# Delta-rule attention and two gated feed-forward layers on one core: seven of sixteen second products in rounded parts, the weights' sign by a steeper negative slope, the second chunk's masks as VectorE products

## The chip, the cores and the metric

One NeuronCore of a Trainium2 chip runs the whole program. The metric is the device time of one execution in microseconds (us). Before the change three runs gave a median of 1096.58 us (1095.71 to 1097.54).

## The reference, cut to what matters

Inputs are q, k, v of shape (4, 8, 768, 48), beta (4, 8, 768), and the weights of two feed-forward layers in 64-bit floats.

```python
k_n = k / (norm(k) + 1e-6)
for t in range(768):                                   # per batch and head
    y[t]  = q[t] @ state
    state = state + beta[t] * outer(k_n[t], v[t] - state.T @ k_n[t])
x = y as (3072 tokens, 384)
h = x @ w_in                                           # layer 1: 384 -> 2048
g = (a0 + a1*h + a2*h**2 + a3*h**3) / (1 + |b0|*|h| + |b1|*h**2 + 1e-6)
x = g @ w_out                                          # 2048 -> 384
h = x @ w_in2; g = max(h, 0)**2; out = g @ w_out2      # layer 2
```

## The kernel before, in words

**Attention** is cut into 12 chunks of 64 time steps by 4 batches: 48 steps n, in six groups of eight (two chunks each). Within a chunk the recurrence is solved by inverting a triangular matrix; that inversion is a chain of 31 pairs of small operations (lines 487 and 491), on VectorE for group 0 and on GpSimd for the others. A step multiplies keys and queries with the state, masks the query-key product to the part above the diagonal, and multiplies on. The mask is made in `middle` (line 679): ScalarE or VectorE copies the product out of PSUM into the tile X (line 691, printed at the helper's lines 345 and 349), and GpSimd zeroes the rest in place (`affine_select`, line 690). X goes into the matmuls of lines 711 and 712.

**The layers** work on six token tiles of 512 columns. A tile has 16 steps j, one for each 128 of the 2048 hidden units. In layer 1 a step is `mm1` (nine matmuls, line 896, into one of three PSUM banks "h"), `rational` (ScalarE, VectorE and one GpSimd product, lines 913 to 923, whose result g goes into one of three buffers) and `mm2_1` (line 933: three products in full fp32, which the trace shows as two matmuls each, added to three PSUM banks over the 16 steps). Layer 2 has the same `mm1`, then `relu2`, then `mm2_2` (lines 957 to 959). There, as in every `mm1`, an operand is split into a rounded part (fp32r) and the remainder, and a product is three matmuls on rounded numbers: high by low, low by high, high by high.

**The weights** come as 64-bit floats, 768 KB per step j and layer, into a "raw" buffer. `weights` (line 811) makes 32-bit floats of them in place: ScalarE scales the high words (line 836, which moves the exponent), VectorE shifts the low words (837), VectorE puts the sign of the high word into the low one (838), VectorE shifts and joins (841 and 843 for layer 1, 847 for layer 2). Then ScalarE rounds (852, 861) and GpSimd forms the remainder (853, 862). In layer 1 eight weights have room of their own and the others share two raw buffers. For layer 2, j = 0 and 1 are loaded into the same two raw buffers in tile 0 and joined early; j = 2 goes into a buffer that exists only after `swap` (line 975), which frees the attention's memory; four lie in quarters of B, once tile 5 of layer 1 has used those for the last time.

**The order of the work** is not the program's text. Every piece of work is a task with an engine, a modelled duration, a due time and its predecessors. `Plan.play` is a list scheduler that simulates all queues, `Plan.late` derives new due times from a simulated schedule, and `Plan.run` takes the best of eight rounds. So each engine's queue is fixed before the chip runs, and each engine works through its queue in order. Constants such as `T0`, `U1` (planned us per step of layer 1), `STEP0`, and the lead of the second layer's weights (100 - 5.5 j us) only set the first due times. `either` leaves a copy to ScalarE or VectorE as the scheduler likes.

Attention of group i+1 and the inversion of group i+2 run beside tile i of layer 1. The prologue, before the first `mm1`, has the attention of group 0 and the inversion of group 1.

Of the kernel before, what the change touches and what calls it, by code (L numbers as in the profile page):

```python
# [19 lines left out]
C = 64  # L20
# [8 lines left out]
N = 2 * CT  # L29
EPS = 1e-6  # L30

T0, U1, U2 = 88.0, 6.0, 4.15
T2 = T0 + 96 * U1 + 3
STEP0, STEP1, INV0, INV1 = 40, 25, -90, -10
GD, GN = 40, 28
ROUNDS, FILL = 8, 0
PREF = 1.0
IV1, WB, WS = 25, 44, 4.5

# [204 lines left out]
def kernel(ctx, tc, kT, kS, qT, kn, vn, beta, par_in, w1, w2, outT):  # L244
# [31 lines left out]
    tiles(one, "raw", 2, [128, 2 * DM], w1.dtype)  # L276
# [33 lines left out]
    mark = at.tile([128, 1, 1], F32, name="mark")  # L310
    be = at.tile([128, 32], F32, name="be")
# [45 lines left out]
    add("POOL", 0.2, lambda: P_.memset(tiny, 1e-30), w=["tiny"])  # L357

# [81 lines left out]
    def attention(g):  # L440
# [238 lines left out]
        def middle(k, due):  # L679
# [3 lines left out]
            for j in range(2):  # L683
# [127 lines left out]
    def weights(l, j, due, duo, slack):  # L811
# [7 lines left out]
        wait = [] if l == 1 or not 1 < j < 8 or j == 3 else [PL.last["late"]] if j < 3 else free2[4 * (j - 4) + 3]  # L819
        over = [i for k in (6, 7) if l == 1 and 4 * (k - 4) <= j < 4 * (k - 3) for i in used["raw", 1, k]]  # L820
        dma(768 if f64 else 384, lambda: raw(rk), src[j], w=[rk, (rk, 1)], due=2 + 2 * j if e and l == 1 else d0 - 10, alloc=None if e else (("raw",), rk), lat=2.2, after=[used["load"]] + wait if l == 2 else [],
# [84 lines left out]
    def rational(i, j, due):  # L906
# [173 lines left out]
```

## Time and profile before

| | us |
|---|---|
| median of three runs | 1096.58 |
| the profiled execution's own time | 1095.48 |
| its span, first to last instruction | 1093.8 |
| TensorE busy | 1034.8 (95%) |
| VectorE, ScalarE, GpSimd busy | 722.0, 615.4, 438.8 |
| mean granted TensorE clock | 0.970 |
| prologue, to the first L896 | about 98 |
| tiles 0 to 5 of layer 1, to the last L933 | 98 to 692.7 |
| layer 2 | 692.7 to the end |

PE is TensorE's matmuls, PEld its weight loads, DVE VectorE, ACT ScalarE, POOL GpSimd, SP the DMA queue. L933 is line 933 of the kernel. The ends of matmuls are modelled, so two that follow each other overlap in the listing: the time of a group is read from the start of one to the start of the next.

### The profile page before, as it was taken

The numbers are of one execution on the slowest core, as the hardware profiler recorded it, in microseconds if no ns is written. First come the engines' busy times: TensorE is split into PE (matmuls) and PEld (weight loads), VectorE is DVE, ScalarE is ACT, GpSimd is POOL, SyncE is SP. The second block draws the span as 40 slices with busy tenths as digits, with TensorE's granted clock in tenths as the row PEclk, the third lists the DMA queues.
The fourth block names the chain that finished last, engine by engine and source line by source line (L and its number), as shares of the span: only waits on it lengthen the run. The fifth ranks groups of instructions, "written<-read, shape, count | busy, mean of one in ns | idle before, by whom it ended". The sixth has DMA issues, their size and how long they took to land.

```text
span 1093.8 us, 22125 instructions
## 1 busy us (share of the span) xinstructions
PE 1034.8 (95%) x8843; PEld 743.4 (68%) x8843; DVE 722.0 (66%) x1164; ACT 615.4 (56%) x1106; POOL 438.8 (40%) x592
## 2 busy tenths in 40 slices
PE   6768898799999999999999899999999999999998
PEld 5656566466666666666666555688888888888886
DVE  4986788799788769767878699894343343433432
ACT  5454776576776777766777588663333232332422
POOL 2398899469628835862232334551000000000000
PEclk7869899899999999999999999999999999999999
DMA  7771536811650381043010321811001010000000
GB/s 238 202 185 54 131 115 205 205 55 38 155 94 34 108 165 47 23 113 64 33 32 8 103 71 31 303 42 47 11 14 44 1 58 1 1 30 1 29 1 29
DMA packets 126022, 85.42 MB, mean 78 GB/s; under 512 B 93344, under 2 KB 110880, under 8 KB 125920
## 3 DMA queue, kind: packets, MB, share of 16 engines
q1 hardware_dynamic: 125920, 84.02, 28.0%
q8 instruction: 69, 1.13, 0.4%
q14 instruction: 33, 0.27, 0.1%
HBM read 64.20 MB, written 18.61 MB: 76 GB/s over the span
## 4 chain that ended last, share of the span: by engine, by line
PE 68%; POOL 10%; DVE 6%; ACT 4%; issue 2%; DMA 1%; SPq 0%; POOLq 0%; ACTq 0%
PE bank L896 31%; PE bank L933 15%; PE bank L959 6%; PE bank L957 6%; PE bank L958 6%; POOL Tt L491 3%; PE bank L652 3%; POOL tmp L487 3%; POOL mem L916 3%; ACT X L345 1%; PE bank L711 1%; POOL A L853 1%; DVE mem L917 1%; DVE mem L350 1%; DVE mem L918 1%
## 5 line engine op out<-in xcount | busy, mean ns | idle before, releaser
L896 PE MATMUL bank<-xh,A 128*128 128x512 f32 x1152 | 361.6, 395 | 3.3 <-POOL A L853 3.3
L933 PE MATMUL bank<-mem,B 128*128 128x512 f32 x576 | 273.1, 607 | 4.6 <-DVE mem L923 4.6
L896 PE MATMUL bank<-xl,A 128*128 128x512 f32 x576 | 257.1, 446 | 15.0 <-DVE mem L923 11.3
L896 PEld LDWEIGHTS bank<-xh,A 128*128 128x128 f32 x1152 | 218.9, 190 | 65.5 <-issue 14.9
L916 POOL TENSOR_TENSOR mem<-mem 128x512 f32<-128x512 f32 x96 | 126.5, 1318 | 186.8 <-ACT mem L914 186.4
L933 PEld LDWEIGHTS bank<-mem,B 128*128 128x128 f32 x576 | 106.5, 192 | 101.2 <-issue 85.7
L945 DVE SCALAR_TENSOR_TENSOR mem<-bank,mem 128x512 f32<-128x512 f32 x96 | 66.2, 689 | 145.9 <-ACT mem L944 145.8
L896 PEld LDWEIGHTS bank<-xl,A 128*128 128x128 f32 x576 | 109.4, 190 | 63.3 <-DVE mem L923 14.7
L944 ACT ACTIVATE mem<-bank 128x512 f32<-128x512 f32 x96 | 57.4, 598 | 147.7 <-PE bank L896 147.7
L957 PE MATMUL bank<-gl,C 128*128 128x512 f32 x288 | 113.6, 395 | 0.5 <-DVE gl L948 0.5
L948 DVE TENSOR_TENSOR gl<-mem,gh 128x512 fp32r<-128x512 f32 x96 | 71.9, 749 | 63.6 <-ACT gh L947 63.4
L959 PE MATMUL bank<-gh,C 128*128 128x512 f32 x288 | 113.8, 395 | 0.0
L958 PE MATMUL bank<-gh,C 128*128 128x512 f32 x288 | 112.0, 389 | 0.0
L947 ACT CAST gh<-mem 128x512 fp32r<-128x512 f32 x96 | 59.6, 621 | 82.9 <-DVE mem L945 71.4
L919 ACT ACTIVATE mem<-mem,par 128x512 f32<-128x512 f32 x96 | 69.3, 722 | 54.4 <-POOL mem L916 53.9
L491 POOL TENSOR_TENSOR Tt<-Tt,tmp 128x31 f32<-128x31 f32 (+15 forms) x155 | 93.6, 604 | 10.8
L921 DVE SCALAR_TENSOR_TENSOR mem<-mem,par,bank 128x512 f32<-128x512 f32 x96 | 71.3, 743 | 38.1 <-ACT bank L920 37.9
L487 POOL TENSOR_TENSOR tmp<-Gb,Tt 128x31 f32<-128x31 f32 (+15 forms) x155 | 88.2, 569 | 14.1 <-DVE Tt L480 3.9
L913 ACT ACTIVATE mem<-bank 128x512 f32<-128x512 f32 x96 | 57.0, 593 | 57.4 <-PE bank L896 42.4
L914 ACT ACTIVATE mem<-mem,par 128x512 f32<-128x512 f32 x96 | 78.0, 813 | 2.7
L345 ACT COPY X<-bank 64x192 f32<-64x192 f32 (+1 forms) x187 | 63.0, 338 | 28.9 <-DVE vn L695 12.9
L917 DVE TENSOR_TENSOR mem<-bank,mem 128x512 f32<-128x512 f32 x96 | 65.9, 687 | 17.7 <-ACT mem L345 15.7
(117 smaller groups left out, 1579.8 us busy)
## 6 DMA issues: line engine op xcount, KB each, us to landing
raw<-in_w_dram SPq DMA_DIRECT2D x18, 768.0 KB, 4.8
B<-in_w_dram SPq DMA_DIRECT2D x10, 768.0 KB, 5.2
kTg<-in_kS_dram SPq DMA_DIRECT2D x40, 128.0 KB, 2.9
gs<-Gs SPq DMA_DIRECT2D x40, 128.0 KB, 2.8
kTc<-in_kT_dram SPq DMA_DIRECT2D x40, 128.0 KB, 2.6
kn<-in_kn_dram SPq DMA_DIRECT2D x12, 384.0 KB, 3.8
X<-in_qT_dram SPq DMA_DIRECT2D x96, 48.0 KB, 2.7
vn<-in_vn_dram SPq DMA_DIRECT2D x12, 384.0 KB, 4.3
```

Of the source, the lines that this page charges most:

```text
L345: A_.copy(a, b) if f is None else A_.mul(a, b, f) if g is None else A_.activation(a, b, AF.Identity, bias=f, scale=g)
L487: E_.tensor_tensor(tv, _mid(Gb[:, s, s + 1:32], [128, a, b]), Tt[:, 0:a, s:s + 1].to_broadcast([128, a, b]), op=ALU.mult)
L491: E_.tensor_tensor(Tt[:, 0:a, s + 1:32], Tt[:, 0:a, s + 1:32], tv, op=ALU.subtract)
L896: M.matmul(h, a, b, start=(k == 0 and m == 0), stop=(k == NK - 1 and m == 2))
L914: add("ACT", 0.83, lambda: A_.activation(b(), a(), AF.Identity, bias=s(4), scale=s(5)), r=[ak, "par"], w=[bk], due=due + 3.3, alloc=(("b", ...
L916: add("POOL", 1.32, lambda: P_.tensor_tensor(b(), b(), a(), op=ALU.mult), r=[ak], w=[bk], due=due + 4.2, lock=1)
L917: add("DVE", 0.69, lambda: V.tensor_tensor(c(), h(), c(), op=ALU.mult), r=[hk], w=[ck], due=due + 5.5)
L933: M.matmul(acc[d], Bw[j][:, 128 * d:128 * d + 128], slot[gk], start=(j == 0), stop=(j == NJ - 1))
L948: add("DVE", 0.72, lambda: V.tensor_tensor(gl(), b(), gh(), op=ALU.subtract), r=[bk, gk, "late"], w=[lk], due=due + 5, lock=1, alloc=(("gl ...
L957: M.matmul(acc[d], wh, gl, start=(j == 0), stop=False)
L958: M.matmul(acc[d], wl, gh, start=False, stop=False)
L959: M.matmul(acc[d], wh, gh, start=False, stop=(j == NJ - 1))
```

## The change

1. For tiles 1 to 5 of layer 1 and the seven steps j in `SJ`, `mm2_1` becomes nine matmuls on rounded parts. ScalarE rounds g (tile ph), GpSimd forms the remainder (tile pl); there is one buffer of each. The weights' parts E and F are made once, in tile 1: seven roundings on ScalarE, seven subtractions on GpSimd. Their memory is that of the two raw buffers and free space, given over by the task `pairs` once all weights of layer 1 are done.
2. The scaling of the high words becomes a parametric ReLU whose negative slope is larger by 2**32. The sign then stands where the later shift by 3 puts it at the top, and the VectorE operation of line 838 goes, for all 32 weights.
3. In chunk 1 (steps n = 4 to 7, in the prologue) one VectorE product of PSUM and a constant triangle `tri` replaces the copy and GpSimd's mask. `tri` is made once on GpSimd.
4. Layer 2 no longer uses layer 1's raw buffers: its weights j < 4 and j > 7 use two new buffers after `swap`, with a planned lead of 60 - 4 j us. `U1` is 5.9 and `STEP0` 36.

```diff
-T0, U1, U2 = 88.0, 6.0, 4.15
+T0, U1, U2 = 88.0, 5.9, 4.15
-STEP0, STEP1, INV0, INV1 = 40, 25, -90, -10
+STEP0, STEP1, INV0, INV1 = 36, 25, -90, -10
+SJ = (1, 3, 5, 8, 10, 12, 14)
+SA, SB = 60, 4
...
+    def corner():
+        P_.memset(tri, 1.0)
+        for o in (0, 64):
+            v = tri[o:o + 64]
+            P_.affine_select(v, v, pattern=[[1, C]], base=0, channel_multiplier=-1, compare_op=ALU.is_gt, fill=0.0)
+    add("POOL", 0.6, corner, w=["tri"], due=14, lock=1)
...
+                if c == 1:
+                    def cp(j=j):
+                        a, y = co(j)
+                        V.tensor_tensor(a, y, _mid(tri[64 * j:64 * j + 64], [64, NP, C]), op=ALU.mult)
+                    add("DVE", 0.38, cp, r=[hk, "tri"], w=[("M", b, j)], due=due, free=[hk])
+                    continue
...
-        wait = [] if l == 1 or not 1 < j < 8 or j == 3 else [PL.last["late"]] if j < 3 else free2[4 * (j - 4) + 3]
+        wait = [] if l == 1 else free2[4 * (j - 4) + 3] if 3 < j < 8 else [PL.last["late"]]
...
-            add("ACT", 0.9, lambda: A_.mul(hi().bitcast(F32), hi().bitcast(F32), 2.0 ** -112), w=[(rk, 1)], due=d0)
+            add("ACT", 0.9, lambda: A_.activation(hi().bitcast(F32), hi().bitcast(F32), AF.Prelu, scale=2.0 ** -112, alpha=2.0 ** 32), w=[(rk, 1)], due=d0)
             add("DVE", 0.62, lambda: V.tensor_scalar(lo(), lo(), 29, None, op0=ALU.logical_shift_right), w=[rk], due=d0, lock=1)
-            add("DVE", 1.0, lambda: V.scalar_tensor_tensor(lo(), hi(), 0x80000000, lo(), op0=ALU.bitwise_and, op1=ALU.bitwise_or),
-                r=[(rk, 1)], w=[rk], due=d0, lock=1)
...
+        if i and j in SJ:
+            pk, mk = ("ph", u), ("pl", u)
+            add("ACT", 0.62, lambda: A_.copy(slot[pk][0], g()), r=[gk, "pairs"], w=[pk], due=due + 10.4, alloc=(("ph",), pk))
+            add("POOL", 1.3, lambda: P_.tensor_tensor(slot[mk][0], g(), slot[pk][0], op=ALU.subtract), r=[gk, pk], w=[mk], due=due + 11.5, lock=1,
+                alloc=(("pl",), mk), free=[gk])
...
+        two = i > 0 and j in SJ
+        if two and i == 1:
+            add("ACT", 0.52, lambda: A_.copy(late["E"][j], Bw[j]), r=[("B", j), "pairs"], w=[("E", j)], due=due - 3)
+            add("POOL", 1.15, lambda: P_.tensor_tensor(late["F"][j], Bw[j], late["E"][j], op=ALU.subtract), r=[("B", j), ("E", j)], w=[("F", j)], due=due - 2, lock=1)
...
+                for m, (a, b) in enumerate(((late["E"][j][:, e], slot[mk][0]), (late["F"][j][:, e], slot[pk][0]), (late["E"][j][:, e], slot[pk][0]))):
+                    M.matmul(acc[d], a, b, start=(j == 0 and m == 0), stop=(j == NJ - 1 and m == 2))
...
+    def pairs():
+        rw.release()
+        sp = tc.alloc_tile_pool(name="sp", bufs=1, side="left", reuse_waits="tile")
...
+    add("POOL", 0.01, pairs, w=["pairs"], due=tm(16) - 4, after=[y for v in used.values() if isinstance(v, list) for y in v])
...
-        late["raw"] = lp.tile([128, 2 * DM], w1.dtype, name="raw2")
+        late["raw"] = [lp.tile([128, 2 * DM], w1.dtype, name=f"raw2_{y}") for y in range(2)]
...
-        weights(2, j, tm(96 + j) - 3, tm(96 + j) + 9, 100 - 5.5 * j)
+        weights(2, j, tm(96 + j) - 3, tm(96 + j) + 9, SA - SB * j)
```

## Rows read from the trace of the kernel before

**Rows 1.** The page's head: span, and TensorE's busy time, share, instructions.

```profile
span 1093.8 us, 22125 instructions
PE 1034.8 (95%) x8843; PEld 743.4 (68%) x8843; DVE 722.0 (66%) x1164; ACT 615.4 (56%) x1106; POOL 438.8 (40%) x592
```

**Rows 2.** Stretches: length, busy PE, PEld, DVE, ACT, POOL (instructions), PEclk, DMA share, GB/s.

```profile
60.00:102.00 42.00, 31.68 (x526) 26.69 (x523) 30.82 (x55) 20.09 (x53) 37.98 (x49) 0.81 0.49 123
102.00:231.20 129.20, 113.27 (x1482) 72.84 (x1480) 102.83 (x167) 90.39 (x158) 99.81 (x133) 0.93 0.56 144
231.20:327.50 96.30, 93.81 (x1074) 59.91 (x1073) 81.43 (x137) 68.45 (x127) 63.99 (x96) 1.00 0.39 91
327.50:425.00 97.50, 96.41 (x1137) 61.64 (x1136) 77.04 (x132) 69.36 (x127) 62.24 (x96) 1.00 0.39 91
425.00:522.40 97.40, 95.69 (x1010) 60.64 (x1009) 73.56 (x123) 67.89 (x122) 61.37 (x96) 1.00 0.25 64
522.40:610.80 88.40, 88.03 (x735) 55.15 (x734) 68.73 (x114) 58.90 (x110) 25.34 (x31) 1.00 0.11 32
610.80:692.70 81.90, 77.05 (x243) 46.37 (x242) 72.79 (x107) 61.73 (x97) 31.13 (x25) 0.98 0.27 94
...
666.00:700.00 34.00, 33.51 (x105) 19.46 (x104) 31.21 (x42) 24.73 (x43) 17.54 (x13) 1.00 0.51 165
...
766.00:832.00 66.00, 66.00 (x289) 54.01 (x289) 24.18 (x37) 22.30 (x38) 0.00 (x0) 1.00 0.07 25
```

**Rows 3.** The chain that ended last, in tile 1: start, us, what.

```profile
300.85 2.07 PE bank L896 x9
302.92 2.57 PE bank L933 x6
```

**Rows 4.** TensorE in the prologue, in order of time: start, us, work [idle before, releaser].

```profile
76.22 1.09 PE L652 MATMUL bank<-vn,TT 64*64 64x48 f32 x16 [0.51 <-DVE vn L695]
82.29 0.45 PE L711 MATMUL bank<-X 112*48 112x64 f32 x2 [4.97 <-POOL X L690]
```

**Rows 5.** GpSimd in the prologue, in order of time, same columns.

```profile
81.83 1.84 POOL L690 TENSOR_SCALAR_AFFINE_SELECT X<-X 64x256 f32<-64x256 f32 x4
```

**Rows 6.** Waits of TensorE in tile 0: in total, times, longest.

```profile
PE bank L896 <- DVE mem L923: 6.2, 3, 4.7
...
PE bank L896 <- POOL A L853: 3.3, 2, 2.1
```

**Rows 7.** Groups over the span: xcount | busy, mean ns | idle before, releaser.

```profile
L947 ACT CAST gh<-mem 128x512 fp32r<-128x512 f32 x96 | 59.6, 621 | 82.9 <-DVE mem L945 71.4 <-PE bank L959 10.9
...
L916 POOL TENSOR_TENSOR mem<-mem 128x512 f32<-128x512 f32 x96 | 126.5, 1318 | 186.8 <-ACT mem L914 186.4
...
L853 POOL TENSOR_TENSOR A<-B,A 128x384 fp32r<-128x384 f32 x10 | 14.0, 1409 | 21.6 <-ACT A L852 21.6
```

**Rows 8.** Waits of ScalarE in tile 1: in total, times, longest.

```profile
ACT mem L919 <- POOL mem L916: 15.6, 13, 2.3
```

**Rows 9.** Groups in the prologue from 60 to 102 us.

```profile
L690 POOL TENSOR_SCALAR_AFFINE_SELECT X<-X 64x256 f32<-64x256 f32 x8 | 3.3, 410 | 1.2 <-POOL X L690 0.5 <-ACT X L345 0.3
...
L729 DVE TENSOR_TENSOR X<-X,bank 48x192 f32<-48x192 f32 x16 | 5.6, 352 | 8.2 <-ACT xin L345 8.0
```

**Rows 10.** Line 838 in tile 0, 122 to 212 us, as a group.

```profile
L838 DVE SCALAR_TENSOR_TENSOR raw<-raw 128x768 uint32<-128x768 uint32 x8 | 9.6, 1201 | 0.7 <-ACT raw L836 0.6
```

**Rows 11.** Line 838 by itself: ns min/median/max, first and last start.

```profile
L838 DVE SCALAR_TENSOR_TENSOR raw<-raw x18: 943/959/1767, 61.1 to 725.5; 128x768 uint32<-128x768 uint32 x18
```

**Rows 12.** ScalarE's scaling of the high words, over the span.

```profile
L836 ACT ACTIVATE raw<-raw 128x768 f32<-128x768 f32 x18 | 16.4, 914 | 0.4 <-DMA raw<-in_w_dram 0.4
```

**Rows 13.** Line 847, layer 2's join, by itself.

```profile
L847 DVE SCALAR_TENSOR_TENSOR raw<-raw x8: 949/1050/1792, 268.3 to 733.5; 128x768 uint32<-128x768 uint32 x8
```

**Rows 14.** GpSimd's longest small product, in order of time.

```profile
94.90 0.60 POOL L491 TENSOR_TENSOR Tt<-Tt,tmp 128x207 f32<-128x207 f32 x1
95.57 2.33 POOL L487 TENSOR_TENSOR tmp<-Gb,Tt 128x192 f32<-128x192 f32 x1
```

**Rows 15.** VectorE at that time.

```profile
95.64 1.21 DVE L479 TENSOR_TENSOR Gb<-Gb,nbr 128x1024 f32<-128x1024 f32 x1
```

More of the change, by code (lines that the diff above doesn't have):

```diff
@@ L275 @@
     f64 = w1.dtype != F32
-    tiles(one, "raw", 2, [128, 2 * DM], w1.dtype)
+    rw = tc.alloc_tile_pool(name="rw", bufs=1, side="left", reuse_waits="tile")
+    tiles(rw, "raw", 2, [128, 2 * DM], w1.dtype)
     early = {j: Ball[:, 1536 * (j - 4):1536 * (j - 3)] for j in (6, 7)}
@@ L285 @@
         slot["raw", 1, j] = words(v)
-    PL.pools["raw"] += [words(Ball[:, 1536 * q:1536 * q + 1536]) for q in range(4)]
+    PL.pool("raw2", [lambda y=y: late["raw"][y] for y in range(2)] + [words(Ball[:, 1536 * q:1536 * q + 1536]) for q in range(4)])
     for q in range(4):
-        slot["raw", 2, 4 + q] = PL.pools["raw"][2 + q]
-        PL.gives["raw", 2, 4 + q] = [("raw", 2 + q)]
-    slot["raw", 2, 2] = lambda: late["raw"]
+        slot["raw", 2, 4 + q] = PL.pools["raw2"][2 + q]
+        PL.gives["raw", 2, 4 + q] = [("raw2", 2 + q)]
     def raw(rk):
@@ L310 @@
     mark = at.tile([128, 1, 1], F32, name="mark")
+    tri = at.tile([128, C], F32, name="tri")
     be = at.tile([128, 32], F32, name="be")
@@ L818, in weights @@
         e = rk in slot
[L819 removed]
+        wait = [] if l == 1 else free2[4 * (j - 4) + 3] if 3 < j < 8 else [PL.last["late"]]
         over = [i for k in (6, 7) if l == 1 and 4 * (k - 4) <= j < 4 * (k - 3) for i in used["raw", 1, k]]
[L821 removed]
+        dma(768 if f64 else 384, lambda: raw(rk), src[j], w=[rk, (rk, 1)], due=2 + 2 * j if e and l == 1 else d0 - 10, alloc=None if e else (("raw" if l == 1 else "raw2",), rk), lat=2.2, after=[used["load"]] + wait if l == 2 else [],
             nb=0 if l == 2 else (3 + 7 * j if j < 3 else WB + WS * (j - 3)))
@@ L932, in go @@
                 begun.append(d)
-                M.matmul(acc[d], Bw[j][:, 128 * d:128 * d + 128], slot[gk], start=(j == 0), stop=(j == NJ - 1))
-            add("PE", 0.85, go, r=[gk, ("B", j)], w=[("acc", d)], due=due + d, free=[gk])
+                e = slice(128 * d, 128 * d + 128)
+                if not two:
+                    M.matmul(acc[d], Bw[j][:, e], slot[gk], start=(j == 0), stop=(j == NJ - 1))
+                    return
+                for m, (a, b) in enumerate(((late["E"][j][:, e], slot[mk][0]), (late["F"][j][:, e], slot[pk][0]), (late["E"][j][:, e], slot[pk][0]))):
+                    M.matmul(acc[d], a, b, start=(j == 0 and m == 0), stop=(j == NJ - 1 and m == 2))
+            if two:
+                add("PE", 0.7, go, r=[pk, mk, ("E", j), ("F", j)], w=[("acc", d)], due=due + d, free=[pk, mk])
+            else:
+                add("PE", 0.85, go, r=[gk, ("B", j)], w=[("acc", d)], due=due + d, free=[gk])
             free2.setdefault(j, []).append(len(PL.tasks) - 1)
@@ L962, in mm2_2 @@
                 out(i, d, due + 0.7 * d + 1, 2)
+    def pairs():
+        rw.release()
+        sp = tc.alloc_tile_pool(name="sp", bufs=1, side="left", reuse_waits="tile")
+        late["sp"] = sp
+        for x in ("E", "F"):
+            late[x] = {j: sp.tile([128, DM], F32R, name=f"{x}{j}") for j in SJ}
+        for x in ("ph", "pl"):
+            PL.pools[x][0].append(sp.tile([128, N], F32R, name=x))
+    for x in ("ph", "pl"):
+        PL.pool(x, [[]])
+    add("POOL", 0.01, pairs, w=["pairs"], due=tm(16) - 4, after=[y for v in used.values() if isinstance(v, list) for y in v])
     LAG1, LAG2 = 15.0, 12.0
@@ L1008 @@
     late["pool"].release()
+    late["sp"].release()
     PLANS.append(PL)
```

2 lines of the change are left out of this document (1 added, 1 removed).

## The prediction

> **What bounds the kernel now.** I read the page's head first: TensorE is busy for 1034.8 of 1093.8 us [rows 1]. Such a mean hides stages, so I cut the span at the ends of the token tiles [rows 2]. The reader is to look for two things: how much of each stretch TensorE leaves idle, and which engine is nearly full there. In tiles 1 to 5 it idles 2.5, 1.1, 1.7, 0.4 and 4.9 us, 10.5 us of 461.5. Layer 2 runs without a gap at 1.00 of the clock. Tile 0 idles 15.9 us of 129.2 at a clock of 0.93, and the 42 us before it 10.3, while GpSimd is busy for 38.0 of them. So TensorE sets the time from 231 us on, and what the change saves of its work there should come back nearly whole; before that, chains through other engines do. Third, the chain that ended last gives the price of a step where nothing is mixed in: nine matmuls of line 896 take 2.07 us, six of line 933 take 2.57 [rows 3]. Last, the waits say what TensorE waited for: in the prologue 5.0 us for a GpSimd mask [rows 4], in tile 0 for g and for weights' remainders [rows 6].
>
> **1. The products in parts.** 35 steps (7 in each of 5 tiles) go from six matmuls to nine rounded ones. In layer 2, 289 matmuls of which nearly all are such ones fill 66.0 us, 0.228 us each [rows 2]; nine are 2.06. A step saves 2.57 - 2.06 = 0.51 us, all of them 17.9 us. The nine weight loads instead of six are in that price, since layer 2 loads once per matmul.
>
> By the Trainium skill (FP8 and Floating Point Precision, TensorE Precision Notes) a full fp32 product is four passes through the array. Four passes of 0.228 us would make 2.74 us of the old three products, a saving of 0.68 us per step and 24 us in all; the trace differs (2.57 us, 3.75 passes), and the row decides.
>
> What it adds beside TensorE: per split step one ScalarE rounding (as line 947, 0.62 us) and one GpSimd subtraction of 512 columns (as line 916, 1.32) [rows 7]; per tile 4.3 and 9.2 us. Tile 2 then has ScalarE at 73.7, GpSimd at 71.5 and VectorE at 77.0 of about 93.9 us: 78, 76 and 82%. VectorE is the fullest; from 666 to 700 us it was busy for 92% and TensorE still for 98.6% [rows 2], so that is bearable. Tile 1 also makes E and F: ScalarE at most 7 x 0.62, GpSimd 7 x 1.41 (as line 853 reading B) [rows 7], so GpSimd gets to 64.0 + 9.2 + 9.9 = 83.1 of 92.7 us, 90%. What hides it: the inversion on GpSimd is for a group whose steps run a tile later. If that cover is gone, F costs up to 9.9 us once.
>
> The split lengthens the way from g to its product by 0.62 + 1.32 = 1.94 us and two handovers. Cover: the scheduler can place one more `mm1` (2.07 us) ahead of the product, since its bank is free once g is made. The new wait is that ph and pl have one buffer each: the rounding waits until the previous split product is done, and behind it on ScalarE stand the next steps' Abs, Ln and Exp, on which VectorE and at last TensorE wait. Split steps lie two or three steps, over 8 us, apart, so the planned wait is short.
>
> I take 16 of the 17.9 us: five tiles with 0.4 us of new waits each, the size of the smallest idle of a tile now. Bounds: all 17.9, or 9, half given back to waits; beyond that, see the slower rival.
>
> **2. The masks.** TensorE ends work at about 77.3 us and starts line 711 at 82.29 after 4.97 us of idle time [rows 4]: GpSimd reaches the masks at 81.83, behind the inversion of group 1 [rows 5]. The change takes 8 masks of 0.41 us from GpSimd (3.3 us) and the eight copies from ScalarE or VectorE, and adds 8 products to VectorE, at 0.35 us for 192 elements [rows 9] and so 0.35 to 0.47 for 256. VectorE has 30.8 busy of 42 us there and loses the sign operations. What is late next: the copies of U on ScalarE, which line 711 needs as well. Making `tri` is three small GpSimd operations early, at nothing: GpSimd is then waiting for group 0's inversion, and if not, the eight masks saved are more. Bounds 0 (something else holds the first `mm1`) to 5 us; I take 4, as the wait is one piece on the path to the first tile.
>
> **3. The signs.** 32 VectorE operations of 0.94 to 1.77 us go [rows 11]. ScalarE's operation keeps its operands and shape; I take the same 0.91 us [rows 12]. Bound below: nothing gained; above: whatever a function that the kernel did not use so far costs around each of its 32 uses. No row prices that; Abs, Identity, Ln, Exp and copies follow each other on ScalarE now with nothing in between, so I give it no term. In tile 0 the eight operations took 9.6 us [rows 10], in a loop over two raw buffers: load, scale, shift, sign, join, round, subtract, load again. TensorE waited 3.3 us for its last link and 6.2 for g, which queues on VectorE with it [rows 6]. Four turns per buffer shorten by 1.2 us each, 4.8; since part of the gap is GpSimd's queue, I take 2, between 0 and 8 (half of tile 0's idle time). In layer 2 sixteen operations go, and TensorE is full there: nothing.
>
> **4. The second layer's weights.** Two loads of 768 KB, their scaling, shifts and joins (line 847 from 268.3 us [rows 13]) move from tiles 0 and 1 behind the swap, to about 595 us. On SP they pass all loads of tiles 1 to 4, which gain; on VectorE tile 1 loses some 6 us of work. Tile 5 gets them, 2 x 1.9 us on VectorE, but loses the signs of six or more weights there at 0.96, so it is no fuller than its 72.8 of 81.9 us [rows 2]. TensorE needs a weight every 4.1 us only from the end of tile 5 on, 75 us after the swap. I cost it at nothing; if that cover were gone, layer 2 would begin late by one weight's passage, some 10 us.
>
> **The sum.** -16 - 4 - 2 = -22 us. Of the profiled execution's own 1095.48 us (span and 1.7 us around it) that leaves 1073.5; the median of the runs shown lies 1.1 us higher, so 1074.6.
>
> **Rivals.**
> - *Dense stretches.* Where no attention is mixed in, steps of 4.65 us become 4.4 on average, and VectorE is fullest in just these. If chains of g then end the wait half the time, the products give 9, the rest 3: 1084.6. For: tile 5, the one with VectorE at 89%, has the largest idle time. Against: the 92% above.
> - *More.* All of 17.9, 5 of the mask wait and 8 in tile 0: 1065.7. For: one GpSimd wait led the prologue's delay, and every shift there moves the inversion too.
> - *Slower: the remainder is late.* The place is GpSimd's queue, the price a wait of TensorE before each split product. ScalarE waits for GpSimd's product 13 times in tile 1, 1.2 us on average [rows 8]. If all 35 products met 1.2 us, that is 42 us against 17.9 and 6: 1114.7. It decides from 0.68 us per product on. For it: GpSimd ran late in the prologue at the same 90%; one small product took 2.33 us instead of about 0.6 [rows 14] while VectorE read two operands from memory beside it [rows 15]. Against: in tiles 2 and 3 GpSimd has 64% and TensorE waits for it for nothing that shows.
>
>   The Trainium skill (SBUF — State Buffer, SBUF: two separate sides) says that GpSimd and a VectorE operation with two inputs in SBUF exclude each other for a whole instruction. By that rule the 42 new subtractions are held up or hold up VectorE; rows 14 and 15 agree with it (2.33 us). But in `rational` most VectorE operations take one input from a bank, and the signs that go are of the kind that blocks, so it stays part of this rival.
> - *Nothing.* The products are cheaper but meet waits of the same size, and the prologue's gain ends at tile 0's weights: 1096.6.
>
> **Chances.** Forecast 0.59, dense 0.20, more 0.10, slower 0.08, nothing 0.03. A measurement can tell 0.2% (2.2 us) from no change; the first three are faster by more: 0.89 faster, 0.03 within, 0.08 slower. The range: from the upper bounds of all three terms, 1065, to the lower bound of the products with nothing from the rest, 1096.6 - 9 = 1087.6, and a little beyond for the dense case, 1089. It leaves out the slower case, nothing, and the edges.
>
> **What would show it.** Right: TensorE's busy time falls by about 18 us; its first L896 starts near 94 us; no mask wait before line 711; tiles 2 and 3 last about 94 us with 1 to 3 us idle; lines 836 keep 0.91 us; layer 2 keeps its gapless pace. Wrong: TensorE waiting for the new subtraction or rounding by more than 0.2 us per split step; VectorE over 92% with TensorE idle; a gap at the start of layer 2 behind line 853 or 862; or a tile 0 as long as before, starting earlier.

## The result, and the profile after

The changed kernel takes 1068.6 us (median of four runs, 1065.81 to 1073.23) where the kernel before takes 1096.22 (1095.71 to 1097.54): a ratio of 0.9747, 95% interval 0.9711 to 0.9783, or 27.6 us less. The forecast was 1074.6. So the sign and the size of the sum were about right. Its shares were not, and the experiments are about that. One run further below, at a granted clock of 0.56, was in a slow state and is left out of the comparison there.

The profiled execution took 1065.81 us. It is the fastest of its four, so stages read from it are up to 3 us better than the median kernel's. First the page's head, which answers to [rows 1]:

```profile
span 1064.1 us, 22303 instructions
PE 1009.4 (95%) x8932; PEld 755.7 (71%) x8932; DVE 711.3 (67%) x1154; ACT 625.6 (59%) x1126; POOL 470.6 (44%) x629
```

TensorE's busy time fell by 25.4 us, nearly the whole difference of the spans (29.7), and its share stayed at 95%. The forecast had about 18 us of it, from the products. Of the 25.4 only 10.4 stand in tiles 1 to 5, where the products are; 8.2 stand in tile 0 and 6.3 in the prologue, and the same matmuls are also busy for longer where the granted clock is lower. The stretches say more. I cut them at the first `mm1`, at the first operation (Abs) on each next tile's h, and at the first operation (Relu) on layer 2's h; the columns are those of [rows 2].

```profile
90.00:203.30 113.30, 104.14 (x1417) 68.22 (x1418) 94.08 (x149) 81.28 (x146) 97.33 (x136) 0.96 0.58 149
203.30:298.70 95.40, 93.36 (x1124) 64.88 (x1124) 80.14 (x135) 74.46 (x139) 77.62 (x110) 0.98 0.40 96
298.70:392.70 94.00, 92.95 (x1203) 66.63 (x1190) 75.99 (x133) 75.34 (x139) 69.53 (x102) 1.00 0.41 94
392.70:488.10 95.40, 92.56 (x1047) 65.10 (x1046) 77.02 (x132) 70.06 (x127) 71.06 (x105) 1.00 0.27 67
488.10:580.05 91.95, 91.06 (x767) 63.15 (x766) 74.02 (x121) 65.93 (x121) 35.15 (x37) 1.00 0.12 37
580.05:666.06 86.01, 76.68 (x263) 50.06 (x262) 77.96 (x109) 62.70 (x99) 38.35 (x32) 0.94 0.29 97
740.00:806.00 66.00, 66.00 (x289) 53.97 (x289) 24.18 (x37) 22.40 (x37) 0.00 (x0) 1.00 0.08 25
```

Tile 0 and tile 5 of the kernel before, cut in the same way:

```profile
98.50:226.90 128.40, 112.37 (x1435) 72.50 (x1436) 101.92 (x162) 86.34 (x153) 100.35 (x134) 0.93 0.56 144
613.50:694.80 81.30, 76.45 (x241) 46.05 (x241) 74.00 (x108) 62.59 (x98) 32.77 (x26) 0.98 0.28 93
```

| us, profiled executions | prologue | tile 0 | tiles 1 to 4 | tile 5 | layer 2 | own time |
|---|---|---|---|---|---|---|
| before | 98.5 | 128.4 | 386.7 | 81.3 | 398.9 | 1095.5 |
| after | 90.0 | 113.3 | 376.8 | 86.0 | 398.0 | 1065.8 |
| difference | -8.5 | -15.1 | -9.9 | +4.7 | -0.9 | -29.7 |

The largest share, 15.1 us, comes from tile 0, where the forecast saw 2. Tile 5, with seven cheaper products, became longer. The waits, the chain and what fills VectorE show why.

The waits of TensorE in tile 5 (line 937 makes g, 910 is `mm1`, 958 the plain second product, 961 the one in parts, 942 the new subtraction):

```profile
PE bank L958 <- DVE mem L937: 8.0, 2, 4.0
PE bank L910 <- DVE mem L937: 1.1, 2, 0.9
PE bank L961 <- POOL pl L942: 0.3, 1, 0.3
```

In the kernel before they were (896 is `mm1`, 923 makes g):

```profile
PE bank L896 <- DVE mem L923: 4.8, 2, 3.9
```

The first of the two waits of 4 us, as stretches ahead of it, in it, and behind it:

```profile
580.05:584.00 3.95, 3.95 (x18) 3.00 (x16) 3.21 (x5) 3.29 (x5) 1.68 (x2) 1.00 0.97 357
584.00:588.00 4.00, 0.09 (x1) 0.00 (x0) 3.93 (x7) 3.76 (x7) 1.17 (x2) 0.94 0.12 48
588.09:591.50 3.41, 3.41 (x5) 1.60 (x6) 3.34 (x6) 1.71 (x4) 1.71 (x2) 0.58 0.00 0
```

Here VectorE is busy for 3.93 of 4.00 us while TensorE stands still. And the wait costs more than its length: in the 3.41 us after it the granted clock is 0.58 (mostly at the lower of the two levels, 1.2 GHz of 2.4), and TensorE does 0.58 x 3.41 = 2.0 us of work there, so it loses another 1.4 us. A wait like this first one stood in the kernel before too: 3.9 us up to 621.46, with a clock of 0.60 behind it. New is the second wait of 4.0 us, up to 653.70, near the end of the tile, with the clock at 0.50 behind it. Before and after:

```profile
621.46:625.70 4.24, 4.24 (x12) 3.02 (x12) 4.24 (x6) 2.85 (x5) 3.60 (x3) 0.60 0.02 4
```

```profile
653.70:658.00 4.30, 4.30 (x5) 1.84 (x6) 4.27 (x8) 0.49 (x2) 1.66 (x2) 0.50 0.27 66
```

Over all of tile 5 the clock is 0.94: 0.06 x 86.0 = 5.2 us, where before it was 0.02 x 81.3 = 1.6.

The chain that ended last, in tile 5, gives the same reading piece by piece (start, us, what):

```profile
597.86 0.81 DVE mem L353
598.67 0.75 DVE mem L935
599.42 0.61 DVE bank L936
600.06 0.69 DVE mem L937
600.75 0.61 DVE mem L931
...
602.13 1.18 DVE raw L853
603.31 0.87 DVE raw L861
```

From 597.86 us to 653.70 it is VectorE's, apart from a few stretches on ScalarE and GpSimd and small gaps: the rational function, and between its operations the shifts (853) and joins (861) of layer 2's weights. Tile 5 is bound by VectorE, not by TensorE.

Two things fill VectorE there (78.0 us instead of 74.0), and the split steps give it no operation of their own. First, the planner leaves it 11 of the tile's 16 copies a2 + a3 h, where it had 5. Before and after:

```profile
L350 DVE TENSOR_SCALAR mem<-bank,par 128x512 f32<-128x512 f32 x5 | 4.0, 807 | 9.9 <-ACT mem L913 9.9
```

```profile
L353 DVE TENSOR_SCALAR mem<-bank,par 128x512 f32<-128x512 f32 x11 | 8.9, 806 | 7.9 <-ACT mem L927 6.6 <-PE bank L910 1.2
```

Second, GpSimd holds the shifts and joins of the weights up. Two operations of GpSimd and the two of VectorE beside them (930 is GpSimd's product in the rational function):

```profile
624.92 1.30 POOL L930 TENSOR_TENSOR mem<-mem 128x512 f32<-128x512 f32 x1 [2.16 <-ACT mem L928]
626.18 1.59 POOL L942 TENSOR_TENSOR pl<-mem,ph 128x512 fp32r<-128x512 f32 x1
```

```profile
625.21 1.43 DVE L853 TENSOR_SCALAR B<-B 128x768 uint32<-128x768 uint32 x1
626.56 2.03 DVE L861 SCALAR_TENSOR_TENSOR raw<-raw 128x768 uint32<-128x768 uint32 x1
```

With no GpSimd operation running at its start, a shift takes 0.55 us and a join 0.95 in this trace. Here the shift ends at 626.64, 0.42 us behind the first GpSimd operation, and the join at 628.59, 0.82 us behind the second. Of the 23 shifts in the whole trace that start while a GpSimd operation is running, 21 end 0.41 to 0.43 us behind it. In tile 5 seven of fifteen shifts and joins are held so, three behind the new subtraction and four behind the product; they take 5.2 us more than free ones would. In the kernel before, the same sum was about 1.0 us.

What the split steps and the scaling cost, as groups over the span:

```profile
L942 POOL TENSOR_TENSOR pl<-mem,ph 128x512 fp32r<-128x512 f32 x35 | 45.4, 1296 | 27.0 <-ACT ph L941 15.3 <-issue 11.2 <-POOL X L700 0.2
L941 ACT CAST ph<-mem 128x512 fp32r<-128x512 f32 x35 | 21.6, 617 | 15.3 <-DVE mem L937 14.9
L852 ACT ACTIVATE raw<-raw 128x768 f32<-128x768 f32 x18 | 16.5, 917 | 0.0
L952 POOL TENSOR_TENSOR F<-B,E 128x384 fp32r<-128x384 f32 x7 | 8.0, 1154 | 0.3 <-ACT E L951 0.3
```

These are the forecast's 1.32, 0.62, 0.91 and (a little less than) 1.41 us [rows 7, 12]. TensorE waits for the new subtraction for 0.3 us in the whole span.

### The profile page after: what moved, and what is told of

Its sections match the earlier page's. It is cut to its first block, busy times and chain, and to the rows that moved or that the text cites. A ratio compares the mean times of both kernels' runs of the same rounds, so it can differ in the third digit from the quotient of the medians.

```text
span 1064.1 us, 22303 instructions
## 1 busy us (share of the span) xinstructions
PE 1009.4 (95%) x8932; PEld 755.7 (71%) x8932; DVE 711.3 (67%) x1154; ACT 625.6 (59%) x1126; POOL 470.6 (44%) x629
## 3 DMA queue, kind: packets, MB, share of 16 engines
q8 instruction: 70, 1.15, 0.4%
## 4 chain that ended last, share of the span: by engine, by line
PE 72%; DVE 13%; POOL 7%; ACT 3%; issue 2%; DMA 2%; SPq 1%; POOLq 0%; DVEq 0%; ACTq 0%
PE bank L910 32%; PE bank L958 10%; PE bank L990 6%; PE bank L988 6%; PE bank L989 6%; PE bank L961 6%; PE bank L662 4%; POOL tmp L497 2%; POOL Tt L501 2%; PE bank L727 1%; DVE mem L937 1%; DVE mem L931 1%; DVE mem L932 1%; DVE mem L935 1%; DVE mem L353 1%
## 5 line engine op out<-in xcount | busy, mean ns | idle before, releaser
L910 PE MATMUL bank<-xl,A 128*128 128x512 f32 x576 | 250.2, 434 | 6.6 <-DVE xl L894 3.4
L958 PE MATMUL bank<-mem,B 128*128 128x512 f32 x366 | 183.0, 621 | 17.4 <-DVE mem L937 17.4
L910 PEld LDWEIGHTS bank<-xl,A 128*128 128x128 f32 x576 | 109.3, 190 | 48.3 <-issue 10.4
L958 PEld LDWEIGHTS bank<-mem,B 128*128 128x128 f32 x366 | 68.2, 194 | 70.2 <-issue 41.8
L501 POOL TENSOR_TENSOR Tt<-Tt,tmp 128x31 f32<-128x31 f32 (+15 forms) x155 | 88.0, 568 | 10.6
L497 POOL TENSOR_TENSOR tmp<-Gb,Tt 128x31 f32<-128x31 f32 (+15 forms) x155 | 84.6, 546 | 14.2 <-DVE Tt L490 4.6
L935 DVE SCALAR_TENSOR_TENSOR mem<-mem,par,bank 128x512 f32<-128x512 f32 x96 | 71.2, 742 | 17.5 <-ACT bank L934 16.5
L928 ACT ACTIVATE mem<-mem,par 128x512 f32<-128x512 f32 x96 | 78.1, 814 | 2.7
L348 ACT COPY X<-bank 64x192 f32<-64x192 f32 (+1 forms) x176 | 59.3, 337 | 27.0 <-PE bank L662 12.4
L932 DVE SCALAR_TENSOR_TENSOR mem<-mem,par,bank 128x512 f32<-128x512 f32 x96 | 71.3, 744 | 4.3 <-ACT mem L927 1.9
```

The lines of the kernel that those rows point to most:

```text
L497: E_.tensor_tensor(tv, _mid(Gb[:, s, s + 1:32], [128, a, b]), Tt[:, 0:a, s:s + 1].to_broadcast([128, a, b]), op=ALU.mult)
L501: E_.tensor_tensor(Tt[:, 0:a, s + 1:32], Tt[:, 0:a, s + 1:32], tv, op=ALU.subtract)
L910: M.matmul(h, a, b, start=(k == 0 and m == 0), stop=(k == NK - 1 and m == 2))
L928: add("ACT", 0.83, lambda: A_.activation(b(), a(), AF.Identity, bias=s(4), scale=s(5)), r=[ak, "par"], w=[bk], due=due + 3.3, alloc=(("b", ...
L932: add("DVE", 0.75, lambda: V.scalar_tensor_tensor(c(), c(), s(1), h(), op0=ALU.add, op1=ALU.mult), r=[hk, "par"], w=[ck], due=due + 6.3)
L935: add("DVE", 0.75, lambda: V.scalar_tensor_tensor(c(), c(), s(0), h(), op0=ALU.add, op1=ALU.mult), r=[hk, "par"], w=[ck], due=due + 8)
```

## The experiments

I first separated the three parts, then the order of the work, then looked for what holds the products back. Line numbers in the traces shift by a few between kernels; g, `mm1` and the others are named beside them. Each ratio is to runs of the kernel before taken beside it (medians of 1096.2 to 1098.3 us). The intervals of the ratios are 2 to 4 us to either side, so a difference between two changed kernels below some 5 us is not clear of the noise; where that matters, the difference of the two ratios is given as well.

### The masks alone

The kernel before, with `tri`, `corner` and the VectorE product for chunk 1, as in the diff above, and nothing else.

```diff
+                if c == 1:
+                    ...
+                    add("DVE", 0.38, cp, r=[hk, "tri"], w=[("M", b, j)], due=due, free=[hk])
+                    continue
```

> The kernel before with the second chunk's masks as VectorE products alone. My forecast's sum: 4 us off (about 1092). Theory A (the early stages): the first line of layer 1 starts 5 to 9 us earlier and tile 0 keeps its length, so 5 to 9 us off (1087 to 1091). Rival B (the masks only shift a wait): tile 0's weights hold the pace anyway, less than 2 us off.

Measured: 1094.56 us against 1097.38, ratio 0.9982 (0.9967 to 0.9998), 2.8 us less. In its profile the first `mm1` starts at 88.0 us, 10.5 earlier than before. But tile 0 lasts 132.4 us (+4.0) and tile 1 99.6 (+4.5). Waits of TensorE in tile 0 (line 867 makes a weight's remainder):

```profile
PE bank L910 <- DVE mem L937: 9.2, 1, 9.2
PE bank L910 <- POOL A L867: 5.5, 2, 4.1
```

The masks did hold the first `mm1`, for more than twice the 4 us that I took. Most of what was gained was then given back, to the waits for g and for the weights' remainders that tile 0 meets all the earlier: a gain at one stage handed back at the next.

### The signs alone

```diff
-            add("ACT", 0.9, lambda: A_.mul(hi().bitcast(F32), ..., 2.0 ** -112), ...)
+            add("ACT", 0.9, lambda: A_.activation(hi().bitcast(F32), ..., AF.Prelu, scale=2.0 ** -112, alpha=2.0 ** 32), ...)
-            add("DVE", 1.0, lambda: V.scalar_tensor_tensor(lo(), hi(), 0x80000000, ...), ...)
```

> The kernel before with the weights' sign made by the steeper negative slope, line 838 gone, nothing else. My forecast's sum: 2 us off (about 1094). Theory A: tile 0 is held by VectorE and the loop over two raw buffers, so it shortens by most of the 15 us that it lost between the two traces: 10 to 15 us off (1081 to 1086), with the prologue as before. Rival B (the new schedule, not the removed operations, shortened tile 0): under 3 us off. Line 836 should keep 0.91 us and no new instruction stand beside it.

Measured: 1082.59 us, ratio 0.988 (0.9852 to 0.9908), 14.8 us less, alone more than any other part. Tile 0 of its profile, beside the row of before above:

```profile
97.60:210.80 113.20, 104.33 (x1320) 67.32 (x1324) 90.42 (x154) 82.27 (x144) 95.74 (x133) 0.98 0.61 161
```

It is 15.2 us shorter: VectorE is busy for 11.5 us less, TensorE idles 8.9 us instead of 16.0, and its clock is 0.98 instead of 0.93. Times the length that is 2.3 instead of 9.0 us lost to the clock. So 7.1 us come from waits and 6.7 from the clock that they had cost; the rest is matmuls that now stand in a neighbouring stage (1320 instead of 1435). All other stages are within 2.1 us of before. My term of 2 us had the idle time only, and of that little.

Two kinds of wait in tile 0 shrank. Those for g fall from 10.4 us (6.2 in [rows 6] and 4.2 in the line of before here) to the 6.6 of the two lines behind it; those for the weights' remainders fall from 3.3 us [rows 6] to none that shows.

```profile
PE bank L933 <- DVE mem L923: 4.2, 1, 4.2
```

```profile
PE bank L894 <- DVE mem L921: 4.7, 2, 3.1
PE bank L931 <- DVE mem L921: 1.9, 2, 1.0
```

### Masks and signs together

Both edits above on the kernel before.

> The kernel before with masks and signs changed, no products, loading and constants as before. Theory A (the two add up): signs alone gave 14 us, masks alone 10 us in the prologue of which tile 0 and 1 took 8 back while line 838 stood there; together 17 to 23 us off, 1074 to 1080. Rival B: as signs alone, 12 to 15 us off, 1082 to 1085.

Measured: 1082.1 us (1080.92 to 1083.99), ratio 0.9861 (0.9838 to 0.9884). That is 0.5 us from the signs alone (2 us by the two ratios), not clear of the noise. The prologue ends 8.9 us earlier than with the signs alone (88.7 against 97.6) and tile 0 is 6.1 longer (119.3 against 113.2). The parts do not add.

### The changed kernel without the masks

`tri`, `corner` and the branch for c == 1 taken out of the changed kernel.

> The changed kernel with the second chunk's masks back on GpSimd. Theory A (the masks' gain is kept once the signs are gone): the first line of layer 1 starts at about 97 us instead of 90 and tile 0 keeps its 113 us, so 5 to 8 us slower than the changed kernel. Rival B (as in the kernel before, tile 0 swallows what the prologue wins): within 3 us of the changed kernel.

Measured: 1074.2 us (1073.43 to 1076.56), ratio 0.9794 (0.9769 to 0.982), 5.6 us more than the changed kernel (5.2 by the two ratios, just clear of the noise). Its wait for the mask in the prologue:

```profile
PE bank L713 <- POOL X L692: 8.8, 1, 8.8
```

The prologue ends at 98.2 us, 8.2 later. So the medians have the masks at 3 us alone, 0.5 on the signs, and 5.6 on the rest of the change. This is one of several places where the same edit has another worth in another order of the work.

### The changed kernel without the products, and the products alone

```diff
-SJ = (1, 3, 5, 8, 10, 12, 14)
+SJ = ()
```

> The changed kernel with no second product in rounded parts (the list of steps empty), the rest as changed. My forecast's sum: 16 us slower than the changed kernel (1084 against 1068). Theory A (the products gave about 5 us, the early stages the rest): 3 to 7 us slower, 1072 to 1076, with tile 5 shorter than the changed kernel's 86.0 us per its own work, near 82. Rival B (all comes from the products): near the kernel before, 1090 or more.

Measured: 1077.74 us (1077.1 to 1080.53), ratio 0.9825 (0.9808 to 0.9843): the products are worth 9.1 us in the changed kernel (8.6 by the two ratios). This kernel differs from the one with both parts above by the loading of layer 2's weights and by the planning constants, and is 3.9 us faster by the ratios (0.9861 and 0.9825). In ratios the whole thus splits into 15.2 us for masks and signs, 3.9 for loading and constants, and 8.6 for the products, 27.7 together.

Tile 5 lasts 84.7 us without the products (591.45 to 676.14). Of the 3.4 more than before the change, 2.1 stand at its end: layer 2's first Relu starts 4.2 us behind the last product instead of 2.1, while TensorE works on. What is left, 82.6 us, is no more than the 82.4 of the kernel with both parts. VectorE is busy for 76.5 us of the 84.7, with 8 of the copies. A wait of 4.0 us for g stands near its start, as in the kernel before. The chain from 585 to 655 us, nearly all of it in tile 5, has TensorE's two lines at 62%, where before they had 87%:

```profile
by line: PE bank L958 34.2%; PE bank L910 28.1%; DVE mem L932 6.0%; DVE mem L931 5.7%; DVE mem L353 5.5%; DVE mem L937 5.0%; DVE mem L935 4.7%; DVE bank L936 4.4%; DVE raw L861 2.9%; ACT mem L927 1.7%; issue 1.1%; DVE B L853 0.7%; DVE raw L
```

```profile
by line: PE bank L933 48.3%; PE bank L896 38.3%; DVE mem L918 2.8%; DVE mem L923 2.0%; DVE mem L921 2.0%; DVE bank L922 1.7%; DVE mem L917 1.7%; DVE raw L838 1.3%; DVE mem L350 1.2%; issue 1.0%; ACT mem L913 0.9%
```

(The second is before's, from 620 to 690 us.) So the chain had moved towards VectorE before any product was split, though TensorE had hardly lost by it (5.0 us idle, 4.9 before). With the products, tile 5 has a second wait for g and lasts 86.0 us.

The changed kernel with the old masks and signs, that is, the products together with the new loading and constants:

> The products in parts with their memory and the second layer's new loading, and the planning constants; signs by line 838 and masks on GpSimd as before. My forecast's sum: 16 us under the kernel before (about 1081). Theory A (in this kernel the products give about 9 us, as the run without them shows, and tile 5 gives some back): 6 to 11 us under it, 1086 to 1091, with tile 5 at 84 us or more against 81.3, and the prologue and tile 0 about as before.

Measured: 1089.64 us (1088.32 to 1090.68) against 1097.62, ratio 0.9927 (0.9906 to 0.9948): 8.0 us. This has the loading and the constants in it, so it prices the products by themselves only if those give nothing here. Both values, 8 and 9, are near my lower bound of 9 and half of what I took.

### The constants of the plan

```diff
-T0, U1, U2 = 88.0, 5.9, 4.15
+T0, U1, U2 = 88.0, 6.0, 4.15
-STEP0, STEP1, INV0, INV1 = 36, 25, -90, -10
+STEP0, STEP1, INV0, INV1 = 40, 25, -90, -10
```

> The changed kernel with the two planning constants of before (6.0 us per step, 40 us lead of the attention's steps). It has the same operations in another order. Theory A: within 3 us of the changed kernel. Rival C (a good part of the gain is the constants' schedule): 5 us or more slower.

Measured: 1076.96 us (1071.82 to 1081.61), ratio 0.9812 (0.9776 to 0.9848), 8.4 us more than the changed kernel with the same operations (7.1 by the two ratios; the four runs spread over 10 us). Tile 0 lasts 127.6 us in its profile (the slowest of its four), at a clock of 0.91, with these waits:

```profile
PE bank L910 <- POOL A L867: 5.5, 5, 2.0
PE bank L958 <- DVE mem L937: 4.4, 1, 4.4
PE bank L910 <- DVE xl L894: 3.5, 1, 3.5
```

The due times of the first plan, in which I saw no term at all, are worth about as much as the seven split products.

### Tile 5: VectorE's copies to ScalarE

If VectorE bounds tile 5, eleven of its operations there can go: the copies a2 + a3 h that the planner left to it. ScalarE has 62.7 of 86.0 us.

```diff
-        either(0.78, 0.7, lambda: (c(), h()), s(2), s(3), ...)
+        if i == NT - 1:
+            add("ACT", 0.78, lambda: A_.activation(c(), h(), AF.Identity, bias=s(2), scale=s(3)), ...)
+        else:
+            either(0.78, 0.7, lambda: (c(), h()), s(2), s(3), ...)
```

> The changed kernel where, in tile 5 alone, the line of a2 + a3 h runs always on ScalarE; in the changed kernel 11 of those 16 were on VectorE at 0.81 us. Theory A (tile 5 is held by VectorE, 78.0 of 86.0 us busy): VectorE loses 8.9 us there and tile 5 shortens by 3 to 5 us, the rest as it was. Rival B (tile 5 waits for its first g and for the chain, not for VectorE's load): less than 1 us, or slower as ScalarE gets fuller.

Measured: 1064.46 us (1063.97 to 1064.65), ratio 0.9698 (0.9679 to 0.9717), 4.1 us less than the changed kernel (5.4 by the two ratios, just clear of the noise). It is the fastest kernel of this study. Tile 5:

```profile
586.30:664.40 78.10, 72.45 (x262) 48.54 (x261) 66.88 (x97) 69.97 (x114) 43.49 (x34) 1.00 0.28 92
```

VectorE goes from 78.0 to 66.9 us, the clock from 0.94 to 1.00, and the tile from 86.0 to 78.1. With the chain above, this shows that VectorE bounded it. The gain is not a fixed one: the two kernels of the last experiment have the same edit, and their tile 5 lasts 82.0 and 82.5 us. VectorE has the same operations there, but is busy for 74.0 and 73.8 us; the shifts, joins and the remainders of x alone take 22.9 and 22.6 us instead of 15.1. Of these 17 operations GpSimd holds up 14 and 13 as shown above, at a cost of some 10 us, where in this kernel it holds 4, at 2.7 us. So where they meet GpSimd is worth about half of what the edit gave to the tile.

The chain of this tile also shows both prices with nothing mixed in, first the product in parts, then the plain one:

```profile
633.08 2.06 PE bank L964 x9
...
637.30 2.58 PE bank L961 x6
```

The difference, 0.52 us, is the forecast's 0.51 per step.

### The same without the products

`SJ = ()` on the kernel of the last experiment: are the products worth their full 17.9 us once tile 5 is relieved?

> The kernel with tile 5's a2 + a3 h on ScalarE, without any product in rounded parts: beside the run with both it prices the products where tile 5 is not held by VectorE. With the products tile 5 took 78.1 us and the whole 1064.5. Theory A (products give nothing in tile 5 only because VectorE holds it): tile 5 at 80 to 82 us here, and 10 to 14 us slower in all, 1074 to 1079. Rival B (the products give about 9 us in any case, by the tiles before): tile 5 at 78 to 79, 1072 to 1074.

Measured: 1073.17 us (1071.19 to 1074.57), ratio 0.9782 (0.9752 to 0.9811). The products are worth 8.7 us here (9.2 by the two ratios), no more than in the changed kernel, though the tile does what was expected. Without and with them:

| us | tiles 1 to 3 | tile 4 | tile 5 |
|---|---|---|---|
| seven steps not split | 288.8 | 95.9 | 81.9 |
| split | 287.2 | 91.9 | 78.1 |
| difference | -1.6 | -4.0 | -3.8 |
| full price, 0.51 each | -10.7 | -3.6 | -3.6 |

Tiles 4 and 5 give the full price; tiles 1 to 3, where GpSimd also runs an inversion, nearly none of it in this pair. There TensorE idles 0.1, 0.3 and 0.7 us without split steps, with them 1.7, 1.8 and 2.8, and the clock is 0.98 in tiles 2 and 3. The idle time (5.1 us more) and the clock (about 3.9) make up the 9.1 us that are missing. Tile 2 without split steps, with them, and in the changed kernel without the masks:

```profile
302.40:399.10 96.70, 96.36 (x1140) 61.85 (x1139) 76.71 (x130) 70.28 (x129) 61.86 (x96) 1.00 0.40 92
```

```profile
300.90:397.20 96.30, 94.49 (x1214) 67.87 (x1201) 75.99 (x133) 75.36 (x138) 69.56 (x102) 0.98 0.41 93
```

```profile
307.80:402.10 94.30, 93.07 (x1172) 65.25 (x1171) 75.06 (x127) 75.33 (x139) 71.33 (x105) 1.00 0.39 96
```

GpSimd goes from 62 to 70 of some 96 us with the split steps, VectorE stays at 76. But GpSimd's load is not what takes the gain: the third row has the same split steps and the same inversion, GpSimd has 71 us in it, and the clock stays at 1.00. In that kernel tiles 1 to 3 last 279.9 us, 9.7 less than the 289.6 of the changed kernel without products, which is nearly the full price; in the changed kernel they last 284.8. With the same operations, the order of the work decides how much of the price comes back.

What TensorE waits for differs as well. In the changed kernel, from tile 1 to the start of tile 5, it is mostly g, and not the remainder of g:

```profile
PE bank L958 <- DVE mem L937: 8.1, 3, 4.0
```

(The 4.0 in it is the wait at 584 us above; about 2 us stand in each of tiles 1 and 3.) In the fastest kernel it is g in tiles 1 and 3 (1.7 and 2.1 us) and a transfer of the attention (the tile TN) in tile 2 (1.8). Which part of the order makes them late is not shown.

### The steeper slope only for layer 1

```diff
+            if l == 1:
+                add("ACT", 0.9, ... AF.Prelu, scale=2.0 ** -112, alpha=2.0 ** 32), ...)
+            else:
+                add("ACT", 0.9, lambda: A_.mul(hi().bitcast(F32), ..., 2.0 ** -112), ...)
...
+            if l == 2:
+                add("DVE", 1.0, lambda: V.scalar_tensor_tensor(lo(), hi(), 0x80000000, ...), ...)
```

> The changed kernel with the steeper slope for layer 1's weights only; layer 2's 16 weights are signed by VectorE as before. My forecast gave layer 2's signs nothing: the same time as the changed kernel, 1067 to 1070. Theory A (tile 5 is held by VectorE, and some eight of these operations of about 1 us fall into it): tile 5 gets 4 to 8 us longer than the changed kernel's 86.0, the total 4 to 9 us slower, 1072 to 1078.

Measured: 1072.97 us (1071.69 to 1073.67), ratio 0.9778 (0.9752 to 0.9805), 4.4 us more than the changed kernel (3.4 by the two ratios), not clear of the noise. I had costed layer 2's signs at nothing. In its profile eight of them stand in tile 5 (9.6 us of VectorE), and the tile is 2.1 us longer, less than the expectation had it; the planner leaves VectorE 6 of the copies there instead of 11. Tile 0 is 8 us longer too, in a profile that is 4.3 us over the changed kernel's median; how much of that is the edit and how much tile 0's own spread stays open.

### Two attempts at tile 0

Both start from the fastest kernel. First, the remainders of five weights of layer 1 go from GpSimd to VectorE:

```diff
+        if l == 1 and j in (1, 2, 3, 4, 5):
+            add("DVE", 0.6, lambda: V.tensor_tensor(Aw[j][:, so], res(si), Aw[j][:, si], op=ALU.subtract), ...)
```

> As the kernel with tile 5's a2 + a3 h on ScalarE, and in addition the remainders of layer 1's weights j = 1 to 5 on VectorE instead of GpSimd. In that kernel TensorE waited 5.9 us in tile 0 for GpSimd's remainder. Theory A (prologue and tile 0 are held by GpSimd's queue): five operations of 1.0 to 1.3 us leave it, the wait goes and tile 0 shortens from 119 to 113 us or less; 1057 to 1061 in all. Rival B (VectorE is as full there): the wait is taken over by one for VectorE; 1063 to 1067.

Measured: 1067.32 us (three runs, 1065.14 to 1070.37; the fourth took 1648.79), ratio 0.9731 (0.9696 to 0.9766). No gain. Tile 0 does get shorter, 112.2 us instead of 119.1, but the prologue ends at 95.3 us instead of 88.0. TensorE no longer waits for GpSimd's remainders, but for the remainder of x on VectorE:

```profile
PE bank L913 <- DVE xl L897: 5.9, 1, 5.9
```

Second, the copies of a2 + a3 h go to ScalarE in tile 0 as well (`if i in (0, NT - 1)`):

> As the kernel with tile 5's a2 + a3 h on ScalarE, now in tile 0 as well (there 9 of the 16 were on VectorE at 0.81 us). Theory A (tile 0, too, is held by VectorE's load, which is why the signs gave so much there): VectorE loses 7.3 us of its 94 in tile 0 and the tile shortens by 3 to 6 us, 1058 to 1062 in all. Rival B (what the signs shortened in tile 0 was the way of the weights, not the load; GpSimd's and ScalarE's queues hold what is left): no shorter than 1063, perhaps longer as ScalarE's roundings of weights queue behind more work.

Measured: 1070.07 us (1068.79 to 1070.42), ratio 0.9749 (0.9724 to 0.9775): slower by 5.6. Tile 0 lasts 123.9 us, VectorE still has 91.0 us in it (93.9 in the kernel it starts from), ScalarE 89 instead of 82, and the waits for remainders are as there (5.5 us where that has 5.9). VectorE was thus relieved by 2.9 us only, so the run does not settle whether a larger relief would help tile 0. That the signs helped it as they did because they stood in the way of each weight, between the load and the remainder, fits the waits above in part, but is not shown: they also took 11.5 us from the engine on which g queues.

## Why the prediction was right or wrong

**The sum.** -22 forecast, -27.6 measured, inside the range. That it fits is partly luck: one term was twice too large, another seven times too small, and a part that had no term gave some 4.

**1. The products, -16 forecast: about -9** (9.1 and 8.7 us in two surroundings, and 8.0 together with the loading and the constants). The price of a step, 0.51 us, was right to the hundredth. By the Trainium skill (FP8 and Floating Point Precision, TensorE Precision Notes) four passes at 0.228 us each would have made it 0.68; the chain in the fastest kernel has 2.58 us for the plain products and 2.06 for nine rounded ones, so the trace differs again. It does not say that there are fewer than four passes: 2.58 us are also twelve passes of 0.215, and no row has a pass by itself, so the 3.75 of the forecast is a price and not a count. What failed is the step "five tiles with 0.4 us of new waits each". The argument for it was that VectorE had been busy for 92% from 666 to 700 us with TensorE hardly waiting [rows 2]. That held only with TensorE as the slower of the two. Steps of 4.65 us that become 4.4 turn it round: in tile 5 VectorE has 78.0 of 86.0 us and heads the chain, with more copies from the planner and with its shifts and joins held up by GpSimd, two things that the step did not count. The rival named dense steps was right in its size, 9, and in its mechanism for tile 5; its time, 1084.6, was wrong, since the other terms were worth more. It did not see tiles 1 to 3, which are not dense and kept 1.6 of 10.7 us in one pair of kernels and 4.8 in the changed one (289.6 to 284.8).

**2. The masks, -4 forecast, between 0 and 5: -3 us alone, -0.5 on the signs, -5.6 in the changed kernel.** The cause was right: no wait for a mask is left ahead of line 727 (711 before), and the first `mm1` starts at 90.0 us, forecast near 94. What failed is to take "one piece on the path to the first tile" as a saving of the whole: tile 0 has its own bounds, the weights and g, and what comes earlier to it waits there. The question "what is late next" was asked for the prologue only.

**3. The signs, -2 forecast, between 0 and 8: -14.8 alone, outside my bounds.** The step that failed is "four turns per buffer shorten by 1.2 us each, 4.8; since part of the gap is GpSimd's queue, I take 2". The loop was the right one. The upper bound was half of the idle time and counted nothing for the clock, though the 0.93 of tile 0 stood in [rows 2]: 0.07 x 129.2 = 9 us lay in it, on top of the 15.9 of idle time. The other half of the term, "in layer 2 sixteen operations go, and TensorE is full there: nothing", may be wrong by up to 4.4 us, within the noise: eight of them stand in tile 5, as my own term 4 said. That the new function costs what the old did (917 against 914 ns) was right.

**4. Layer 2's weights, nothing forecast: 3.9 us less by the ratios, together with the new constants and without products**. The constants by themselves move some 8 us in the changed kernel, so it may be theirs; no run prices the loading alone. In tile 5 they show no loss (82.6 and 82.4 us up to where layer 2 begins). What failed is "no fuller than its 72.8 of 81.9 us": cut at the same places, VectorE has 74.0 us before and 78.0 after. The signs that go (7.0 us) were more than made up by six more copies (4.9) and by the shifts and joins, which grow from 10.5 to 16.1 us, 4.1 of it from being held up.

**The order of the work** had no term, and the two constants alone move some 8 us. A change that goes through a planner comes with a new order everywhere; the range allowed for that, but no step of the working did.

**The slower rival** fell: TensorE waits 0.3 us in all for the remainder of g (2.6 in the fastest kernel), far under the 0.68 us per product from which it would have decided. Its neighbour rule, from the Trainium skill (SBUF — State Buffer, SBUF: two separate sides), has GpSimd and a VectorE operation with two inputs in SBUF exclude each other for a whole instruction. The trace agrees, on the side of VectorE: the joins, which read two operands, end 0.82 us behind the GpSimd operation beside them, and the shifts, which read one, 0.42. That costs about 5.2 us of VectorE's time in tile 5. The subtractions themselves took 1.30 and 1.15 us where the nearest rows of before had 1.32 and 1.41. The forecast put the price on the subtraction and on TensorE's wait for it; it falls on the engine that makes g.

**Layer 2** kept its gapless pace as forecast: 66.00 of 66.00 us, and the waits behind tile 5 name none of TensorE's.

## What to carry to other kernels

Before you give an engine less to do, look in each stage for the engine that is fullest after it, and ask there, not only at the edit, what is late next. Price a wait of TensorE together with the granted clock of its stretch. Look for operations whose time differs from one use to the next, and at what runs beside the long ones. Where a planner orders the work and may place it, see what it moved onto the full engine, and run the change with the old planning constants too, or the worth of the order is booked to the edit.

## What the runs showed that I had not expected

- A wait of 4.0 us was followed by 3.4 us at a granted clock of 0.58. In the kernel before, a wait of 4.7 us was followed by 7.2 us at 0.66, which the second row shows (112.1 to 119.3 us; the row before it is the wait):

```profile
107.00:112.10 5.10, 0.46 (x5) 0.17 (x2) 4.54 (x7) 3.53 (x4) 4.88 (x8) 0.81 0.17 68
112.10:119.30 7.20, 7.13 (x16) 4.60 (x17) 2.77 (x6) 2.99 (x6) 5.00 (x10) 0.66 0.77 203
```

  The second is 0.34 x 7.2 = 2.4 us of work lost behind 4.7 us of wait.
- The changed kernel's four runs spread over 7.4 us and those of the fastest kernel over 0.7. Between the two profiles tile 0 differs by 5.8 us (113.3 and 119.1), though the edit is in tile 5 alone; the planner orders all of the work anew for it. So single profiles do not settle a few microseconds of tile 0, and what makes the one kernel steadier was not found.
